# Attention and a feed-forward layer on one core: block products by seven instead of eight for the last 3072 tokens

## The chip, the cores and the metric

The kernel runs on one core of one Trainium2 chip. The metric is the device time of one execution in microseconds (us). The core has a matrix engine (TensorE, "PE"; its weight loads are listed apart as "PEld"), VectorE ("DVE"), ScalarE ("ACT"), GpSimd ("POOL") and SyncE ("SP"), which issues all the transfers of this kernel. Each engine works through its own queue in the order in which the program gives it instructions, and waits there for what an instruction needs.

## The reference

Eight batches of 576 tokens pass through attention with eight heads of width 64. Four heads look at the last 32 positions, four at the positions of the same residue modulo 32. The result, 4608 tokens by 512, goes through two matrix products with a gate between them.

```python
mask_local = (rel >= 0) & (rel < stride)                       # stride = 32
mask_strided = (rel >= 0) & (pos[None, :] % stride == pos[:, None] % stride)
...
x = attn_out.transpose(0, 2, 1, 3).reshape(B * S, H * D)       # 4608 x 512
h = x @ w_in                                                   # 512 x 2048
g = np.where(h >= 1, h, np.where(h <= -1, 0.0, (h + 1) ** 2 / 4))
return g @ w_out                                               # 2048 x 512
```

Everything is float32. The kernel gets that precision from a fast matmul type of fewer bits by splitting each operand into a high and a low part and adding three products: high by high, high by low, low by high (`HI_LO`).

## The kernel before

**Tiles.** The feed-forward layer runs over nine chunks `c` of 512 tokens, and in each over 16 blocks `f` of 128 hidden columns. `up(c, f)` makes one block of `h` by 12 matmuls of 128x128 weights against 512 tokens (four blocks of the 512 inputs by three products, line 540). `gate` makes `g` from it: a Relu with scale and bias on ACT (549), a square on ACT (550), `max(h, 1)` against that, the smaller one, on DVE (554), then the high part on ACT (556) and the low part on DVE (559). `down` adds the block into four output banks by 12 matmuls (570). All 16 blocks of both weights lie in SBUF in split form for the whole run; they are split during chunk 0 (lines 172 to 203, on ACT, DVE and POOL).

**PSUM.** Four banks hold the output sums ("o"), two the blocks of `h` ("h"), two serve attention ("a").

**Attention.** One batch is a list of named steps on four units `u`: scores `s` on PE, mask `m` and maximum `x` on DVE, `a` (subtract the maximum) on POOL (368), exponential `e` on ACT (375), sum `q` on DVE (379), `p` (add epsilon) on ACT (383), `r` (reciprocal on DVE, then a multiplication on POOL, 392), `t` (transposes of 32x32 blocks on DVE, 429), `j` (eight transfers to DRAM and one back, 443 and 444, on SP), values `v` on PE, and the high and low parts of the result, `h` on ACT (500) and `l` on DVE (504), which are written into the ring `xT` of 1536 tokens.

**Order.** The order is written out by hand, for every engine. Batches 0 and 1 are spread by `begin` and `STEPS` over the start and chunk 0. From chunk 1 on one batch is spread by `LATER` over the 16 blocks of a chunk, so that seven chunks have a batch beside them (0 to 6) and the last two none. From chunk 1 on `down` runs for two blocks at once, after the `up` of every even block: PE sees up, down of two blocks, up, up, down of two blocks, up. The gate of an odd block has the time of one `up` before its result is used.

## Time and profile before

Three runs took 881.39, 881.96 and 882.36 us (median 881.96). The profiled execution has a span of 881.9 us from its first to its last instruction, which is its own time.

| what | value |
|---|---|
| span of the profiled execution | 881.9 us |
| PE busy | 872.9 us, 99% |
| DVE busy | 384.6 us, 44% |
| ACT busy | 398.0 us, 45% |
| POOL busy | 114.7 us, 13% |
| mean granted PE clock | 0.996 of full |
| moved by DMA | 77.61 MB, mean 88 GB/s |

Busy times are sums over instructions. PE's is modelled: the end of a matmul lies after the start of the next one, so that what a matmul costs is better read from the distance of starts than from its mean duration.

### The profile page before, as it was taken

To read this page: it belongs to the slowest core of one execution; us is meant where nothing else is said; L and a number is where in the kernel's file an instruction comes from. 1 tells how busy PE (TensorE), PEld (TensorE's weight loads), DVE (VectorE), ACT (ScalarE), POOL (GpSimd) and SP (SyncE) were. 2 spreads that over 40 slices of the span, in tenths; PEclk is the share of its full clock that TensorE was granted. 3 is DMA by queue.
4 is the path that set the end of the run, shared out by engine and by line. 5 is a ranking of instruction groups with operands and counts; after the bars stand their busy time and mean duration, and the time that the engine had idled before them with its cause. 6 is when DMAs were issued, how large, how long until landed. Compare 5 with 4: busy or idle time off the path is not lost.

```text
span 881.9 us, 17353 instructions
## 1 busy us (share of the span) xinstructions
PE 872.9 (99%) x7253; PEld 710.3 (81%) x7253; DVE 384.6 (44%) x709; ACT 398.0 (45%) x732; POOL 114.7 (13%) x136
## 2 busy tenths in 40 slices
PE   8999999999999999999999999999999999999998
PEld 6788888888888888887888888888888888888886
DVE  5899854443453434434344345333453322222221
ACT  5889953434434443334434343444333433343333
POOL 6354411100120002100110011100210000000000
PEclk8999999999999999999999999999999999999999
DMA  9917331422232322421241223321222000000001
GB/s 354 405 65 242 114 121 61 140 59 60 105 100 81 83 70 72 125 64 62 81 145 52 67 105 94 87 82 49 76 82 60 33 29 1 0 35 14 1 0 48
DMA packets 41646, 77.61 MB, mean 88 GB/s; under 512 B 8800, under 2 KB 22112, under 8 KB 41568
## 3 DMA queue, kind: packets, MB, share of 16 engines
q1 hardware_dynamic: 41568, 76.50, 26.8%
q8 instruction: 57, 0.93, 0.4%
q14 instruction: 21, 0.17, 0.1%
HBM read 59.18 MB, written 17.30 MB: 87 GB/s over the span
## 4 chain that ended last, share of the span: by engine, by line
PE 95%; DMA 1%; ACT 1%; DVE 1%; SPq 1%; issue 0%; ACTq 0%; DVEq 0%
PE o L570 44%; PE h L540 44%; PE xp L459 3%; PE sc L302 3%; DMA qk<-in_qk_s 1%; PE tp L405 1%; SPq L443 0%; DMA pT<-there 0%; ACT u L549 0%; ACT u L550 0%; DMA there<-t 0%; DVE xTl L504 0%; DVE h L554 0%; SPq L237 0%; ACT gh L556 0%
## 5 line engine op out<-in xcount | busy, mean ns | idle before, releaser
L540 PE MATMUL h<-xTh,w 128*128 128x512 f32 x1152 | 373.2, 391 | 0.4 <-DVE u L554 0.4
L570 PE MATMUL o<-w,gh 128*128 128x512 f32 x1152 | 359.5, 393 | 0.1
L554 DVE SCALAR_TENSOR_TENSOR h<-h,u 128x512 f32<-128x512 f32 x143 | 100.0, 699 | 377.1 <-ACT u L550 377.0
L540 PEld LDWEIGHTS h<-xTh,w 128*128 128x128 f32 x1152 | 216.3, 188 | 46.6 <-DVE u L554 0.8
L570 PEld LDWEIGHTS o<-w,gh 128*128 128x128 f32 x1152 | 213.4, 188 | 45.3 <-ACT gh L556 0.6
L540 PE MATMUL h<-xTl,w 128*128 128x512 f32 x576 | 224.5, 390 | 0.4 <-DVE xTl L504 0.4
L570 PE MATMUL o<-w,gl 128*128 128x512 f32 x576 | 224.9, 390 | 0.0
L549 ACT ACTIVATE u<-h,half 128x512 f32<-128x512 f32 x144 | 99.1, 688 | 269.6 <-PE h L540 268.6
L559 DVE TENSOR_TENSOR gl<-h,gh 128x512 fp32r<-128x512 f32 x143 | 98.9, 692 | 84.6 <-ACT gh L556 83.7
L570 PEld LDWEIGHTS o<-w,gl 128*128 128x128 f32 x576 | 108.1, 188 | 25.7 <-DVE gl L559 0.6
L540 PEld LDWEIGHTS h<-xTl,w 128*128 128x128 f32 x576 | 108.1, 188 | 22.9 <-DVE xTl L504 1.1
L556 ACT CAST gh<-h 128x512 fp32r<-128x512 f32 x128 | 75.2, 587 | 100.1 <-DVE h L554 100.1
L550 ACT ACTIVATE u<-u 128x512 f32<-128x512 f32 x144 | 91.0, 632 | 4.6
L368 POOL TENSOR_TENSOR pr<-pr,st 128x768 f32<-128x768 f32 (+3 forms) x31 | 36.3, 1172 | 322.8 <-DVE st L364 307.6
L392 POOL TENSOR_TENSOR pr<-pr,st 128x648 f32<-128x648 f32 (+3 forms) x30 | 35.2, 1173 | 119.3 <-DVE st L391 118.4
L191 POOL TENSOR_TENSOR raw<-raw 128x512 uint32<-128x512 uint32 (+1 forms) x34 | 35.0, 1047 | 37.9 <-DVE raw L186 23.4
L504 DVE TENSOR_TENSOR xTl<-xp,xTh 128x216 fp32r<-128x216 f32 (+8 forms) x94 | 35.7, 442 | 6.0 <-ACT xTh L500 6.0
L383 ACT ACTIVATE st<-st 128x12 f32<-128x12 f32 (+2 forms) x32 | 6.8, 211 | 67.5 <-DVE st L379 67.4
L459 PEld LDWEIGHTS xp<-pT,v 64*64 64x64 f32 (+2 forms) x1760 | 29.0, 138 | 10.1 <-issue 8.2
L302 PEld LDWEIGHTS sc<-qk 64*32 64x32 f32 (+1 forms) x1856 | 25.9, 117 | 12.1 <-issue 10.1
L459 PE MATMUL xp<-pT,v 64*64 64x32 f32 (+2 forms) x1760 | 32.3, 224 | 1.5 <-DMA pT<-there 0.8
L500 ACT CAST xTh<-xp 128x216 fp32r<-128x216 f32 (+8 forms) x94 | 31.1, 459 | 6.0 <-DVE xTl L504 3.5
(56 smaller groups left out, 348.3 us busy)
## 6 DMA issues: line engine op xcount, KB each, us to landing
raw<-in_w SPq DMA_DIRECT2D x30, 512.0 KB, 9.6
qk<-in_qk_s SPq DMA_DIRECT2D x16, 604.0 KB, 4.9
qk<-in_qk_l SPq DMA_DIRECT2D x16, 576.0 KB, 4.8
out<-ob SPq DMA_DIRECT2D x35, 256.0 KB, 2.0
v<-in_v_l SPq DMA_DIRECT2D x21, 384.0 KB, 4.0
there<-t SPq DMA_DIRECT2D x96, 48.0 KB, 1.7
pT<-there SPq DMA_DIRECT2D x12, 384.0 KB, 3.0
v<-in_v_s SPq DMA_DIRECT2D x7, 384.0 KB, 4.4
```

Source lines behind the costliest of these rows:

```text
L302: nc.tensor.matmul(sc[j][i * Q:(i + 1) * Q, s, p], qk[:, 0, q0:q0 + Q], qk[:, 1, k0:k0 + W], start=u not in covered, stop=u not in covered)
L368: eng.tensor_tensor(out=pr, in0=pr, in1=st[:, 0].unsqueeze(2).broadcast_to(list(pr.shape)), op=ALU.add)
L392: eng.tensor_tensor(out=pr, in0=pr, in1=st[:, 2].unsqueeze(2).broadcast_to(list(pr.shape)), op=ALU.mult)
L459: nc.tensor.matmul(xp[p][j * D:(j + 1) * D, n], loaded[b, local, b0 + n][keys, j], qs, start=True, stop=True)
L504: nc.vector.tensor_tensor(out=dst[1], in0=src, in1=dst[0].bitcast(F32), op=ALU.subtract)
L540: nc.tensor.matmul(o_ps[c, f], wt[f][:, x, 0, cc * P:(cc + 1) * P], xT[y][:, cc, r0:r0 + CH], start=first and n == 0, stop=last and n == l ...
L549: nc.scalar.activation(u, hp, AF.Relu, bias=half, scale=0.5)
L550: nc.scalar.activation(u, u, AF.Square)
L554: nc.vector.scalar_tensor_tensor(out=g, in0=hp, scalar=1.0, in1=u, op0=ALU.max, op1=ALU.min)
L556: nc.scalar.copy(gh, g)
L559: nc.vector.tensor_tensor(out=gl, in0=g, in1=gh.bitcast(F32), op=ALU.subtract)
L570: nc.tensor.matmul(o_ps[c][t], gs[x][:, t * P:(t + 1) * P], wt[f][:, y, 1, :], start=f == 0 and n == 0, stop=f == NF - 1 and n == 2)
```

## The change

The 4608 tokens are taken as three plain chunks of 512 (`CLASSIC = 3`, c = 0, 1, 2, as before, with all weights in SBUF) and three blocks `s` of 1024 tokens.

**Blocks of 1024.** In a block both products are done by Winograd's form of Strassen's scheme: inputs and weights are cut into 2 by 2 blocks, seven products `m` of sums of blocks stand for the eight products of blocks. `up_block` goes over eight pairs `j` of hidden blocks. For each it makes seven products of 6 matmuls, in the order 1, 2, 3 of the pair before, 6, 4 of the pair before, 5, 7 (`UP`, 56 products). It adds them up in three PSUM banks (y, x, z; two sets, for even and odd `j`) and in SBUF, and puts the gate of four blocks of `g` between the products. `down_block` has 28 steps of 12 matmuls (`DOWN`), products 1, 2, 6, 7, 5, 3, 4 in this order, each over four quarters `k` of the hidden width. Before each step `prep` makes the sum of blocks of `g` where one is needed and splits it into high and low part (`split`: copy on ACT, subtraction on DVE, 1024 columns each).

**Weights.** The sums of weight blocks are made once, in chunks 1 and 2: `ship` writes three of the four split blocks of a pair to DRAM, and `combine` makes the four sums: six additions on POOL, the high part on ACT, the low part on DVE, and one transfer of 1 MB to DRAM. There are 16 combines (8 for each weight), at f = 0, 1, 2, 4, 5, 6, 8, 9, 10 of chunk 1 and f = 4, 5, 7, 8, 9, 11, 12 of chunk 2. They share one buffer `st` (and one `w32`). In the blocks each product's weights, 256 KB, come back from DRAM into a ring of seven tiles (`fetch_w`), each issued on SP when the product that used its tile is done.

**Inputs.** `x_sum` (DVE) and `x_split` (ACT and DVE) make the seven operands of a block of tokens: those of the first block in chunk 2, those of the others in the down steps of the block before (`X_NEXT`).

**Attention.** Batches start at fixed places counted in quarters of an `f`, or products (`START`), and take 42 of these instead of 64: batches 2, 3, 4 and part of 5 run in chunks 1 and 2, the rest of 5 and most of 6 in the up part of the first block, 7 in the up part of the second. The tokens of one batch are now cut at every multiple of 512 below 1536 and at 1536, 2560 and 3584.

**Output.** In `down` the weights become the stationary operand and `g` the moving one, so that the output is made transposed, 512 by 4608, and turned back on the host by a plain transposition. SBUF is given out in named slots that weights, ring, operands and blocks of `g` use one after another.

The core of the diff:

```diff
-_OUTS = [((4608, 512), "float32")]
+_OUTS = [((512, 4608), "float32")]
...
+    def combine(i, j, w32, st):
+        for f in range(2):
+            parts = [wt[2 * j + f][:, i, :, x].bitcast(F32) for x in range(2)]
+            nc.gpsimd.tensor_tensor(out=w32[:, 2 * f:2 * f + 2], in0=parts[0], in1=parts[1], op=ALU.add)
...
+        for to, a, b, op in ((0, block(1, 0), block(1, 1), ALU.add), (1, s_[0], block(0, 0), ALU.subtract),
+                             (2, block(0, 0), block(1, 0), ALU.subtract), (3, block(0, 1), s_[1], ALU.subtract)):
+            nc.gpsimd.tensor_tensor(out=s_[to], in0=a, in1=b, op=op)
+        hi, lo = st[:, :, :HF], st[:, :, HF:]
+        nc.scalar.copy(hi.bitcast(F32R), lo.bitcast(F32))
+        nc.vector.tensor_tensor(out=lo.bitcast(F32R), in0=lo.bitcast(F32), in1=hi.bitcast(F32), op=ALU.subtract)
+        nc.sync.dma_start(kept[i][j][1].rearrange("p n x e -> p n (x e)"), st)
...
     def down(*units):
...
-                    nc.tensor.matmul(o_ps[c][t], gs[x][:, t * P:(t + 1) * P], wt[f][:, y, 1, :],
+                    nc.tensor.matmul(o_ps[c][d], wt[f][:, 1, h, x, e:e + P], gs[y],
...
+    def fetch_w(n):
+        if n < len(seq):
+            i, j, m = seq[n]
+            ring[n] = short(RING_AT[n % WR], F32R, f"wr_{n}", (P, 2, HF))
+            which, at = FACTOR[m]
+            nc.sync.dma_start(ring[n].bitcast(F32), kept[i][j][which][:, at])
...
+        for n, (j, m) in enumerate(UP):
...
+            for c in range(2):
+                for q, (a, b) in enumerate(HI_LO):
+                    nc.tensor.matmul(to, w_[:, a, c * P:(c + 1) * P], xc[m][:, b, c],
...
+            fetch_w(done - 1 + WR)
+            if m == 1:
+                last = (gb[(j - 1) // 2][:, 1, (j - 1) % 2], tmp[j - 1][:, 1]) if j else None
+                if last:
+                    bent(last[1], last[0])
+                nc.scalar.copy(g11, y[j])
+                if last:
+                    squared(last[1])
+                    gated(last[0], *last)
+            elif m == 2:
+                nc.vector.tensor_tensor(out=g11, in0=x.pop(j), in1=g11, op=ALU.add)
+                bent(ua, g11)
+                squared(ua)
+            elif m == 3:
+                nc.vector.tensor_tensor(out=g12, in0=z.pop(j), in1=g12, op=ALU.add)
+                bent(ub, g12)
+            elif m == 6:
+                nc.scalar.copy(g12, y[j])
+                gated(g11, g11, ua)
+                if j:
+                    last = ga[(j - 1) // 2][:, 1, (j - 1) % 2], tmp[j - 1][:, 1]
+                    squared(last[1])
+                    gated(last[0], *last)
+            elif m == 4:
+                h = y.pop(j)
+                bent(ua, h)
+                squared(ua)
+                gated(g21, h, ua)
...
+    def prep(s, n):
+        m, k = DOWN[n]
+        hl[n] = t = slot(HL_AT[n % 3], [P, 2, 2, CH], F32R, f"hl_{s}_{n}")
+        b11, t3, b21, b22 = ga[k][:, 0], ga[k][:, 1], gb[k][:, 0], gb[k][:, 1]
+        if m == 5:
+            nc.vector.tensor_tensor(out=t3, in0=b22, in1=b11, op=ALU.subtract)
+        elif m == 4:
+            nc.vector.tensor_tensor(out=b21, in0=b21, in1=b11, op=ALU.subtract)
+        split(t, {1: b11, 6: b11, 5: t3, 7: t3, 3: b22, 2: b21, 4: b21}[m])
...
+        START = {2: 0, 3: 33, 4: 69, 5: 112, 6: 150, 7: 240}
+        LATER = {0: ("s0", "m0 x0 a0"), 3: ("", "e0"), 6: ("s1", "q0 p0 r0 m1 x1 a1"), 9: ("", "t0 j0 e1"),
+                 12: ("s2", "q1 p1 r1 m2 x2 a2"), 15: ("", "t1 j1 e2"), 18: ("v0", "h0 l0"),
+                 21: ("s3", "m3 x3 a3 q2 p2 r2"), 24: ("", "t2 j2 e3"), 28: ("", "q3 p3 r3"),
+                 33: ("v2", "h2 l2 t3 j3"), 42: ("V1", "h1 l1 h3 l3")}
```

More of the change, by code (lines that the diff above doesn't have):

```diff
@@ L140, in tile_sparse_attention_then_ffn, with x_tile @@
     nc.gpsimd.memset(half, 0.5)
-    xT = [const.tile([P, NC, RING], F32R, name=f"xT{s}") for s in "hl"]
+    xq = [slot(f"X{c}", [P, 2, NC, CH], F32R, f"xq_{c}") for c in range(2)]
+    xs = {}
+    def x_tile(s):
+        if s not in xs:
+            xs[s] = slot(f"X{s % 2}", [P, NC, 2 * CH], F32, f"xs_{s}")
+        return xs[s]
     wt, raws, pieces, held = {}, {}, {}, set()
@@ L560, in gate, with put @@
         return gh, gl
+    def put(rows, cols, t):
+        nc.sync.dma_start(out[rows * P:(rows + 1) * P, cols:cols + CH], t)
     def down(*units):
@@ L571, in down @@
                                      start=f == 0 and n == 0, stop=f == NF - 1 and n == 2)
             if f1 == NF - 1:
-                end = (c, t) == (NCH - 1, CH // P - 1)
-                for e, cols in enumerate((slice(0, 384), slice(384, DM)) if end else (slice(0, DM),)):
-                    n = cols.stop - cols.start
-                    ob = (s_p if end else o_p).tile([P, n], F32, tag="s" if end else "ob", name=f"ob_{c}_{t}_{e}")
-                    nc.scalar.copy(ob, o_ps[c][t][:, cols])
-                    nc.sync.dma_start(out[c * CH + t * P:c * CH + (t + 1) * P, cols], ob)
+                ob = o_p.tile([P, CH], F32, tag="ob", name=f"ob_{c}_{d}")
@@ L666, in tile_sparse_attention_then_ffn @@
                         fetch_qk(2, 0)
-                if post:
-                    go(post)
-                n = 2 if 0 < c and (c, f) < (NCH - 1, NF - 1) else 1
+                go(post)
+                if c:
+                    steps(g0, g0 + 2, 1)
+                    ship(f, c - 1)
+                    if (c, f) in COMBINE:
+                        i, j = COMBINE[c, f]
+                        if c == 1:
+                            w32, st = (x_tile(0)[:, :, e0:e1] for e0, e1 in ((704, 960), (192, 704)))
+                        else:
+                            w32, st = (slot(X_AT[m], [P, 4, n], F32, f"{a}_{j}") for m, n, a in ((3, HF, "w32"), (4, CH, "st")))
+                        combine(i, j, w32, st)
+                    if c == 2:
+                        x_steps(0, *X_FIRST.get(f, ()))
+                n = 2 if c else 1
                 if len(pend) > 2:
```

309 lines of the change are left out of this document (253 added, 56 removed), and 3 rows, old and new, of the table LATER.

## The prediction

> **What bounds the kernel now.** First the page: busy shares, bytes per slice, the four large matmul groups.
>
> ```profile
> span 881.9 us, 17353 instructions
> PE 872.9 (99%) x7253; PEld 710.3 (81%) x7253; DVE 384.6 (44%) x709; ACT 398.0 (45%) x732; POOL 114.7 (13%) x136
> ...
> GB/s 354 405 65 242 114 121 61 140 59 60 105 100 81 83 70 72 125 64 62 81 145 52 67 105 94 87 82 49 76 82 60 33 29 1 0 35 14 1 0 48
> ...
> L540 PE MATMUL h<-xTh,w 128*128 128x512 f32 x1152 | 373.2, 391 | 0.4 <-DVE u L554 0.4
> L570 PE MATMUL o<-w,gh 128*128 128x512 f32 x1152 | 359.5, 393 | 0.1
> ...
> L540 PE MATMUL h<-xTl,w 128*128 128x512 f32 x576 | 224.5, 390 | 0.4 <-DVE xTl L504 0.4
> L570 PE MATMUL o<-w,gl 128*128 128x512 f32 x576 | 224.9, 390 | 0.0
> ```
>
> PE is never short of work. The means overlap, so I take a matmul's price from the chain of waits in order of time, and that of a chunk from windows over line 570, one with an attention batch beside it and one without.
>
> ```profile
> 782.08 5.44 PE h L540 x24
> ```
> ```profile
> 172.97:268.98 96.01, 45.41 (x193) 1.00 0.29 85
> 782.08:869.40 87.32, 45.05 (x193) 1.00 0.03 13
> ```
>
> A matmul costs 5.44/24 = 0.2267 us, an up or a half of a down (12) 2.72, a batch 96.0 - 87.3 = 8.7 us of PE. Then the timeline of one gate, which shows how much room there is:
>
> ```profile
> 781.92 0.39 PE L540 MATMUL h<-xTh,w 128*128 128x512 f32 x1
> ...
> 784.90 0.69 ACT L549 ACTIVATE u<-h,half 128x512 f32<-128x512 f32 x1 [5.47 <-PE h L540]
> ...
> 786.28 0.70 DVE L554 SCALAR_TENSOR_TENSOR h<-h,u 128x512 f32<-128x512 f32 x1 [6.13 <-ACT u L550]
> ...
> 787.02 0.59 ACT L556 CAST gh<-h 128x512 fp32r<-128x512 f32 x1 [0.76 <-DVE h L554]
> ...
> 787.64 0.69 DVE L559 TENSOR_TENSOR gl<-h,gh 128x512 fp32r<-128x512 f32 x1 [0.66 <-ACT gh L556]
> ...
> 788.38 0.19 PEld L570 LDWEIGHTS o<-w,gl 128*128 128x128 f32 x1
> ```
>
> The odd block's up ends at 781.92 + 2.72 = 784.64; ACT starts 0.26 later and the gate takes 3.4 (784.90 to 788.33). PE fetches the low part at 788.38, as it appears: an odd gate has no slack. An even one has until the second next up, 8.16 - 0.26 - 3.4 = 4.5 us.
>
> **What is removed.** Before: 1152 + 1152 + 576 + 576 = 3456 matmuls. After: three chunks of 384 and three blocks of 56 x 6 + 28 x 12 = 672, together 3168. 288 fewer are 65.3 us; attention's matmuls stay. With everything else hidden: 881.9 - 65.3 = 816.6. The rest asks how much of this the queues give back.
>
> **The combines (chunks 1 and 2).** Prices of the new shapes come from the groups by form:
>
> ```profile
> L392 POOL TENSOR_TENSOR pr<-pr,st 128x768 f32<-128x768 f32 x7 | 10.3, 1476 | 5.5 <-DVE st L391 5.5
> L392 POOL TENSOR_TENSOR pr<-pr,st 128x384 f32<-128x384 f32 x7 | 5.8, 834 | 36.6 <-DVE st L391 36.6
> ```
> ```profile
> L201 DVE TENSOR_TENSOR w<-raw,w 128x512 fp32r<-128x512 f32 x30 | 19.4, 684 | 0.0
> L392 DVE TENSOR_TENSOR pr<-pr,st 128x768 f32<-128x768 f32 x1 | 1.0, 957 | 0.0
> ```
> ```profile
> L550 ACT ACTIVATE u<-u 128x512 f32<-128x512 f32 x144 | 91.0, 632 | 4.6
> L375 ACT ACTIVATE pr<-pr 128x768 f32<-128x768 f32 x8 | 6.8, 846 | 2.0 <-POOL pr L368 2.0
> ```
>
> By straight lines: POOL 0.62 us for 256 columns and 1.05 for 512; 1024 columns 1.23 on DVE, 1.06 on ACT. For the transfers (KB, us to landing; then one spread `j` on SP's timeline, whose last row is the price of one issue):
>
> ```profile
> out<-ob SPq DMA_DIRECT2D x35, 256.0 KB, 2.0
> ...
> qk<-in_qk_s SPq DMA_DIRECT2D x16, 604.0 KB, 4.9
> ```
> ```profile
> 177.94 3.61 SPq L443 DMA_DIRECT2D there<-t  x8
> 182.92 0.34 SPq L444 DMA_DIRECT2D pT<-there  x1
> ```
>
> 1 MB lies between 2.0 us plus 768 KB at the page's 405 GB/s (3.9) and 4.9 in proportion (8.3); I take 4.5, because the 604 KB loads go out in pairs that share the engines. There is one `st`, so the combines form a ring: copy on ACT 1.06, low part on DVE 1.23, issue 0.35, landing 4.5, four POOL additions 2.5, handovers 0.3, together 9.9 us. The copy stands in ACT's queue ahead of the next gate, and PE waits for that. A block `f` lasts 87.3/16 plus 3.4 batches x 8.7 over 32 blocks: 6.4 us. The first combine also waits on POOL for `a0` (1.48), two additions (2.1) and four (2.5), then copies: 7.1 behind its gate. Chunk 1: 7.1 + 8 x 9.9 = 86 against 10 blocks, 64: 22 late, less the 4.5 an even gate may wait: 18. Chunk 2: 7.1 + 6 x 9.9 = 66 against 8 blocks, 51: less 4.5, 11. So at least some 29. Laying the queues out block by block, with odd gates that have no slack and with combines behind `a` and `r` of the same slot, I get 41 for chunk 1, and 7/9 of it, 32, for chunk 2. From below: a landing of 3.9, queued POOL work done early and both gates tolerant leave 10. I take 40 of 10 to 73, nearer 29, since the layout takes each wait at its longest.
>
> **Up parts.** Gate prices, besides the 632 above:
>
> ```profile
> L554 DVE SCALAR_TENSOR_TENSOR h<-h,u 128x512 f32<-128x512 f32 x143 | 100.0, 699 | 377.1 <-ACT u L550 377.0
> ...
> L549 ACT ACTIVATE u<-h,half 128x512 f32<-128x512 f32 x144 | 99.1, 688 | 269.6 <-PE h L540 268.6
> ...
> L556 ACT CAST gh<-h 128x512 fp32r<-128x512 f32 x128 | 75.2, 587 | 100.1 <-DVE h L554 100.1
> ```
>
> Seven products are 9.52 us of PE. Product 1 of pair j+1 overwrites the bank that the gate after product 4 of j-1 reads. Following ACT and DVE from product 1 (1.36, then 0.26): copy, square, gated, sum, bent, square, bent, copy, square, bent, square, gated is 2 x 0.59 + 4 x 0.63 + 2 x 0.70 + 0.69 + 2 x 0.63 + 0.69 = 7.7 and twelve handovers of 0.03: 9.7 us. So a bare period loses 0.2, 4 over 21 periods (0 to 6).
>
> Attention comes on top, about 2.45 batches in the up parts (0.6, 0.85, 1). Its groups on ACT, and ACT's wait for DVE inside it from the view of waits (us, times, longest):
>
> ```profile
> L375 ACT ACTIVATE pr<-pr 128x768 f32<-128x768 f32 (+3 forms) x32 | 22.2, 694 | 2.0 <-POOL pr L368 2.0
> ...
> L383 ACT ACTIVATE st<-st 128x12 f32<-128x12 f32 (+2 forms) x32 | 6.8, 211 | 67.5 <-DVE st L379 67.4
> ...
> L500 ACT CAST xTh<-xp 128x216 fp32r<-128x216 f32 (+8 forms) x94 | 31.1, 459 | 6.0 <-DVE xTl L504 3.5
> ```
> ```profile
> ACT st L383 <- DVE st L379: 67.4, 26, 4.0
> ```
>
> Per batch 60.1/8 = 7.5 us of work, and 67.4/26 = 2.6 us of waiting at each of four `p`: up to 18 us in a queue that is now PE's clock, against the 8.7 that PE has for itself. That is 0 to 9 a batch, 0 to 23; I take half, 12.
>
> **Weights from DRAM.** A tile is issued when a product ends and is needed six products later, 8.16 us; less 0.35 and 2.0 for landing 5.8 remain. Ahead of it on SP now stand the spreads. By the two rows of SP above one holds it for 5.3 us (177.94 to 183.26), after it has waited for DVE's transposes. Ten fall into up parts (batch 5 two, 6 and 7 four each). With 2.5 us for the transposes each is 2 late, less attention's own PE time: 0 to 25 in all, I take 5, because a PE that is late for other reasons gives the ring its time.
>
> **Down parts.** A step is 2.72 us. For products 5 and 4 `prep` is serial, sum, copy, low part: 1.23 + 1.06 + 1.23 + 0.1 = 3.6. Four steps of product 5 with one sum and one split for the next block between them take 17.0 of DVE against 10.9; the steps before leave a lead of 1.8: 4.3 lost in two blocks, 0.5 in the last. Product 4 with two output sums: 16.0 against 10.9, lead 3.3: 1.8 in each. Together 14 (6 to 20). Where up turns to down, the third operand waits for the last gate (its slot is `tmp`): 1.4 a block; with the first ring tiles and the two early splits, 6 (2 to 12).
>
> **Small parts.** Batch 0 is now cut at token 512: eight more high parts in the start, where PE waits for them.
>
> ```profile
> L500 ACT CAST xTh<-xp 128x36 fp32r<-128x36 f32 x12 | 3.5, 288 | 0.0
> ```
>
> 8 x 0.29 = 2 us (0 to 4). In `down` the low part is needed one matmul earlier, 0.23 a pair; most of it lies inside the combines' stalls: 1 (0 to 4). The split order of the weights and the transposed output change no count.
>
> **Sum.** 816.6 + 40 + 4 + 12 + 5 + 14 + 6 + 2 + 1 = 900.6. The median stands 0.06 above the span: 901 us, 19 more than before.
>
> **Rivals.** *The queues hold (faster).* If the combines' ring is shorter than a block and a third (8.5 us: landing 3.9 and POOL additions that start while the transfer runs), PE never feels them. For it speaks that DVE and ACT stand at 44% and 45%; against it, that one buffer is waited for by three engines in turn. Then 10 remain of the 40, and of the other 44 about half, since PE's own lateness then no longer piles up from stage to stage: 816.6 + 10 + 22 = 849. The sign turns where all stalls together reach 65.
>
> *The clock falls.* My layout leaves PE idle for 4 to 8 us before odd gates. At the start PE had a thin stretch, and the granted clock (the number behind the brackets) followed:
>
> ```profile
> 14.00:16.00 2.00, 1.03 (x8) 0.82 (x8) 2.00 (x5) 1.98 (x5) 0.66 (x1) 1.00 1.00 377
> ...
> 18.00:20.00 2.00, 1.70 (x31) 1.23 (x27) 0.64 (x3) 1.41 (x4) 0.65 (x1) 0.50 1.04 422
> ...
> 22.00:24.00 2.00, 2.00 (x12) 1.96 (x11) 1.95 (x5) 1.07 (x4) 0.74 (x1) 0.65 1.04 417
> ```
>
> Some 6 us at half clock lose 3. Ten such gaps are 30, of which a part lies in stalls anyway: 901 + 25 = 926. [...]
>
> *The ring starves.* Spreads, loads of q, k and v and 193 GB/s of tiles (256 KB per 1.36 us) share one queue: at the upper ends of ring and attention, 901 + 20 + 11 = 932. Against it: the page's 405 GB/s.
>
> *The matmuls don't get fewer in time.* If changing banks every six matmuls or streaming `g` costs what is saved, 0.02 us on each of 3168 matmuls, 63 us: 882 if no queue stalls. The up of today changes its bank every 12 without loss.
>
> **Chances.** Forecast 0.42 (885 to 915), queues hold 0.27 (835 to 879), clock 0.17, ring 0.10, no gain on PE 0.04. Under 0.2% (1.8 us) this kernel's runs tell nothing. Faster 0.28, the first rival and a little; same 0.03; slower 0.69. The range takes in most of the first rival and reaches the two slow ones: 843 to 938; the forecast's own is 885 to 915.
>
> **What would show it.** Right: in the windows of chunks 1 and 2, 384 matmuls take 20 us more than 96; ACT's copy in `combine` waits for POOL, POOL's third addition for the transfer; in down, DVE's low part waits for ACT and PE for DVE. Wrong: a chunk with combines at 96 us; PE waiting for ring tiles above all; a granted clock under 1 in chunks 1 and 2; products that start more than 1.36 us apart in the last block.

## The result, and the profile after

The kernel after took 988.14 us (median of 4, 987.04 to 992.65) beside 881.67 us (881.27 to 882.36) for the kernel before: 1.121 times the time, 95% interval 1.119 to 1.124, or 106 us more. The forecast was 901 us, its range 843 to 938: the sign was right, the size was not.

First the page of the kernel after: span, busy times, and in the slices PE's busy share and granted clock in tenths.

```profile
span 985.3 us, 17928 instructions
PE 857.5 (87%) x6965; PEld 679.3 (69%) x6965; DVE 555.8 (56%) x822; ACT 495.7 (50%) x852; POOL 236.7 (24%) x244
...
PE   8999967767698865868889798998889989999997
...
PEclk8999988969799997989999899999999999999999
```

The 288 matmuls are gone (7253 to 6965), yet the span grew. PE has holes in slices 6 to 27 above all, and its clock dips there too; from slice 34 on it is as dense as before. In windows by stage this is chunks 1 and 2 (first row), the up parts of the three blocks (the next three, the third without attention), and then five rows of 2 us around the first combine. After the length of the window stand PE, PEld, DVE, ACT and POOL, each busy time with the number of instructions, then granted clock, DMA share and GB/s.

```profile
124.60:436.30 311.70, 234.65 (x2270) 183.13 (x2268) 127.85 (x212) 105.52 (x197) 128.06 (x133) 0.87 0.53 174
441.90:551.40 109.50, 95.95 (x985) 74.35 (x985) 60.55 (x102) 65.83 (x118) 20.70 (x16) 0.96 0.75 244
639.50:741.70 102.20, 91.97 (x801) 72.00 (x800) 52.05 (x87) 59.22 (x105) 17.42 (x13) 0.95 0.65 199
825.00:901.50 76.50, 76.47 (x338) 63.03 (x337) 37.98 (x55) 52.48 (x87) 7.22 (x3) 1.00 0.68 200
...
136.00:138.00 2.00, 0.71 (x4) 0.24 (x2) 0.00 (x0) 0.00 (x0) 1.92 (x3) 1.00 0.00 0
138.00:140.00 2.00, 0.00 (x0) 0.00 (x0) 0.00 (x0) 0.00 (x0) 1.92 (x4) 1.00 0.00 0
140.00:142.00 2.00, 0.00 (x0) 0.00 (x0) 0.24 (x1) 1.32 (x2) 1.92 (x3) 0.50 0.00 0
...
152.00:154.00 2.00, 1.60 (x3) 1.07 (x4) 1.37 (x2) 1.29 (x2) 0.00 (x0) 0.50 0.00 0
...
156.00:158.00 2.00, 2.00 (x8) 1.59 (x7) 1.90 (x6) 0.86 (x2) 2.00 (x2) 0.73 1.03 357
```

From 124.6 us on, chunks 1 and 2 hold 31 ups of 2.72 us, 17 double downs of 5.44 and 3.4 batches of 8.7, together 206. They took 312: 105 us lost, where the prediction had 40. An up part has 56 products of 1.36, 76.2 us, and 8.7 for each batch beside it (1.45, 1 and none); beyond that the three lost 26 (with 5.6 between the last plain matmul and the first product), 17 and 0.3 us. The down parts took 88.1, 83.2 and 79.7 against 76.2, which is 22 more. 816.6 + 105 + 43 + 22 is 987, within 2 of the span.

The timeline of the first combine (start, duration, engine, line; in brackets the wait just before and its releaser; some rows in between left out) shows what a late sum does:

```profile
133.68 3.03 PE L599 MATMUL h<-xq,w 128*128 128x512 f32 x12
133.74 1.47 POOL L409 TENSOR_TENSOR pr<-pr,st 128x768 f32<-128x768 f32 x1 [19.62 <-PE sc L343]
135.17 2.52 POOL L244 TENSOR_TENSOR xs<-w 128x512 f32<-128x512 f32 x2
137.76 2.88 POOL L252 TENSOR_TENSOR xs<-xs 128x256 f32<-128x256 f32 x4
140.68 1.04 ACT L254 CAST xs<-xs 128x1024 fp32r<-128x1024 f32 x1 [9.73 <-POOL xs L252]
141.63 1.55 ACT L644 COPY ob<-o 128x512 f32<-128x512 f32 x3
141.75 1.32 DVE L255 TENSOR_TENSOR xs<-xs 128x1024 fp32r<-128x1024 f32 x1 [8.16 <-ACT xs L254]
142.26 0.80 PE L640 MATMUL o<-gh,w 128*128 128x512 f32 x1 [5.56 <-ACT ob L644]
143.10 0.62 SPq L256 DMA_DIRECT2D ks<-xs  x1
143.82 5.55 SPq L629 DMA_DIRECT2D out<-ob  x4
147.76 2.89 POOL L252 TENSOR_TENSOR xs<-xs 128x256 f32<-128x256 f32 x4 [3.56 <-DMA ks<-xs]
148.43 0.58 ACT L644 COPY ob<-o 128x512 f32<-128x512 f32 x1 [5.25 <-DMA out<-ob]
151.76 0.58 ACT L622 CAST gh<-h 128x512 fp32r<-128x512 f32 x1 [0.77 <-DVE h L609]
152.40 0.80 PE L640 MATMUL o<-gh,w 128*128 128x512 f32 x1 [8.49 <-ACT gh L622]
```

ACT stands 9.73 us at the combine's copy. Behind it are the copies that empty the output banks of chunk 0, and PE waits 5.56 us for a bank. The four output transfers stand in SP's queue behind the combine's 1 MB, which waits for DVE; the last `ob` copy waits 5.25 for a free buffer, the next gate stands behind it, and PE waits 8.49 us more. One combine cost 14 us of PE time. From 136.71 PE was idle; from 140 the clock is at half, and after 152.4 it took until about 157 to come back: the fall came 3.3 us after PE stopped, and the return 4.7 us after it went on.

A much shorter hole of this trace, too, was followed by a fall: PE stood for 2.03 us (294.80 to 296.83), and the clock was at half from 297.0 to 300.4. In rows of 2 us, PE's busy time and the granted clock (1.00, 1.00, 0.55, 0.59, 1.00):

```profile
292.80:294.80 2.00, 2.00 (x9) 1.31 (x7) 0.00 (x0) 0.00 (x0) 0.00 (x0) 1.00 0.62 228
294.80:296.80 2.00, 0.00 (x0) 0.00 (x0) 0.00 (x0) 1.79 (x4) 0.00 (x0) 1.00 0.28 101
296.80:298.80 2.00, 1.72 (x96) 1.49 (x96) 0.74 (x2) 1.64 (x3) 0.00 (x0) 0.55 0.99 296
298.80:300.80 2.00, 2.00 (x16) 1.56 (x6) 1.35 (x3) 0.58 (x1) 0.00 (x0) 0.59 0.47 130
300.80:302.80 2.00, 2.00 (x10) 1.62 (x10) 1.97 (x4) 0.07 (x1) 0.00 (x0) 1.00 0.21 43
```

In the whole stretch PE was idle for 311.70 - 234.65 = 77 us; busy time times (1 - clock) over windows of 2 us gives another 23 lost to the clock. The kernel before has neither in the same 312 us of its time:

```profile
124.60:436.30 311.70, 310.93 (x2692) 253.34 (x2694) 129.37 (x245) 127.29 (x234) 33.02 (x33) 1.00 0.28 86
```

The view of waits of the kernel after (us, times, longest):

```profile
ACT xs L254 <- POOL xs L252: 51.8, 8, 11.3
...
ACT st L254 <- POOL st L252: 36.0, 6, 9.7
...
PE o L640 <- ACT gh L622: 23.1, 7, 8.5
...
PE sc L343 <- DVE xq L563: 16.7, 3, 9.8
...
PE xp L500 <- DMA pT<-there: 11.4, 2, 9.9
...
PE z L722 <- DMA wr<-ks: 8.2, 3, 3.3
PE y L722 <- DMA wr<-kq: 7.3, 2, 5.6
PE y L722 <- DMA wr<-ks: 7.2, 3, 2.9
```

ACT stood 88 us at the copies of 14 combines. PE waited not only for gates (23.1) but also with attention's own matmuls at the head of its queue: scores for a bank (16.7), values for the spread probabilities (11.4). What the new instructions cost, by form, and what the new transfers took to land:

```profile
L244 POOL TENSOR_TENSOR xs<-w 128x512 f32<-128x512 f32 x18 | 25.7, 1449 | 0.2
L252 POOL TENSOR_TENSOR xs<-xs 128x256 f32<-128x256 f32 x36 | 25.6, 731 | 12.5 <-DMA ks<-xs 11.3
```
```profile
kq<-w SPq DMA_DIRECT2D x48, 256.0 KB, 4.0
ks<-xs SPq DMA_DIRECT2D x9, 1024.0 KB, 5.3
ks<-st SPq DMA_DIRECT2D x7, 1024.0 KB, 5.0
```

### The profile page after: what moved, and what is told of

Its sections match the earlier page's. It is cut to its first block, busy times and chain, and to the rows that moved or that the text cites. A ratio compares the mean times of both kernels' runs of the same rounds, so it can differ in the third digit from the quotient of the medians.

```text
span 985.3 us, 17928 instructions
## 1 busy us (share of the span) xinstructions
PE 857.5 (87%) x6965; PEld 679.3 (69%) x6965; DVE 555.8 (56%) x822; ACT 495.7 (50%) x852; POOL 236.7 (24%) x244
## 4 chain that ended last, share of the span: by engine, by line
PE 44%; DVE 16%; DMA 12%; ACT 11%; POOL 9%; issue 5%; SPq 3%; ACTq 0%; DVEq 0%; POOLq 0%
PE y L722 9%; PE yo L828 8%; PE h L599 6%; PE o L640 6%; DMA wr<-ks 5%; PE z L722 4%; DVE hl L691 4%; PE xo L828 3%; ACT hl L690 3%; PE xp L500 2%; POOL xs L252 2%; PE x L722 2%; SPq L484 2%; POOL st L252 2%; DMA there<-t 2%
## 5 line engine op out<-in xcount | busy, mean ns | idle before, releaser
L722 PE MATMUL y<-x,wr 128*128 128x512 f32 x576 | 148.1, 404 | 20.2 <-DMA wr<-kq 7.3
L640 PE MATMUL o<-gh,w 128*128 128x512 f32 x384 | 134.9, 418 | 28.7 <-ACT gh L622 23.1
L599 PE MATMUL h<-xq,w 128*128 128x512 f32 x576 | 148.8, 410 | 3.7 <-DVE gl L625 2.8
L722 PEld LDWEIGHTS y<-x,wr 128*128 128x128 f32 x576 | 109.7, 194 | 49.6 <-DVE gb L609 6.2
L828 PE MATMUL yo<-hl,wr 128*128 128x512 f32 x576 | 136.9, 395 | 7.4 <-DVE hl L691 4.7
L599 PEld LDWEIGHTS h<-xq,w 128*128 128x128 f32 x576 | 111.8, 198 | 30.2 <-DVE gl L625 3.2
L828 PEld LDWEIGHTS yo<-hl,wr 128*128 128x128 f32 x576 | 108.6, 190 | 34.0 <-DVE hl L691 7.8
L640 PEld LDWEIGHTS o<-gh,w 128*128 128x128 f32 x384 | 76.7, 200 | 49.3 <-ACT gh L622 26.4
L722 PE MATMUL z<-x,wr 128*128 128x512 f32 x288 | 75.8, 400 | 8.3 <-DMA wr<-ks 8.2
L640 PE MATMUL o<-gl,w 128*128 128x512 f32 x192 | 79.7, 415 | 1.1 <-DVE gl L625 1.1
L343 PE MATMUL sc<-qk 64*32 64x64 f32 (+1 forms) x1856 | 35.6, 242 | 23.7 <-DVE xq L563 16.7
L500 PE MATMUL xp<-pT,v 64*64 64x32 f32 (+2 forms) x1760 | 35.2, 234 | 22.1 <-DMA pT<-there 11.4
```

The lines of the kernel that those rows point to most:

```text
L343: nc.tensor.matmul(sc[j][i * Q:(i + 1) * Q, s, p], qk[:, 0, q0:q0 + Q], qk[:, 1, k0:k0 + W], start=u not in covered, stop=u not in covered)
L500: nc.tensor.matmul(xp[p][j * D:(j + 1) * D, n], loaded[b, local, b0 + n][keys, j], qs, start=True, stop=True)
L599: nc.tensor.matmul(o_ps[c, f], wt[f][:, 0, h, x, e:e + P], xq[c][:, y, cc], start=first and n == 0, stop=last and n == len(todo) - 1)
L640: nc.tensor.matmul(o_ps[c][d], wt[f][:, 1, h, x, e:e + P], gs[y], start=f == 0 and n == 0, stop=f == NF - 1 and n == 2)
L722: nc.tensor.matmul(to, w_[:, a, c * P:(c + 1) * P], xc[m][:, b, c], start=m in (1, 2, 5) and c + q == 0, stop=c == 1 and q == 2, skip_grou ...
L828: nc.tensor.matmul(to, w_[jj][:, a, d * P:(d + 1) * P], t[:, b, jj], start=m in (1, 2, 5) and k + jj + q == 0, stop=k == NP // 2 - 1 and j ...
```

## The experiments

All start from the kernel after. Each was run twice beside three runs of the kernel before (medians 881 to 883 us), the last, e20, five times beside eight. Stages are read from the first matmul of each in the timeline: "plain" is chunks 1 and 2, from 124.6 us in every run. The first matmul of chunk 1 lay between 118.3 and 120.7 us, so that differences of some 2 us in that column can come from ahead of it.

| run | us | ratio to before, 95% | plain | up, down of block 0 | block 1 | block 2 |
|---|---|---|---|---|---|---|
| after | 988.1 | 1.119 to 1.124 | 312 | 109.5, 88.1 | 102.2, 83.2 | 76.5, 79.7 |
| e1_late_end | 980.3 | 1.103 to 1.121 | 308 | 111.4, 90.1 | 99.7, 83.0 | 76.5, 79.7 |
| e5_sums_stay | 968.4 | 1.089 to 1.104 | 291 | 112.1, 88.3 | 100.2, 83.0 | 76.5, 79.7 |
| e11_late_and_stay | 931.3 | 1.052 to 1.061 | 254 | 114.0, 88.3 | 99.9, 83.0 | 76.5, 79.6 |
| e2_no_sums | 925.1 | 1.044 to 1.054 | 246 | 111.6, 90.0 | 103.7, 83.3 | 76.5, 80.0 |
| e10_few_bytes | 907.1 | 1.017 to 1.038 | 231 | 115.2, 89.2 | 100.4, 83.0 | 76.5, 79.7 |
| e14_few_bytes_slots | 900.6 | 1.017 to 1.023 | 224 | 115.1, 88.2 | 98.8, 83.0 | 76.5, 79.6 |
| e3_gate_ring | 979.0 | 1.106 to 1.115 | 300 | 115.0, 88.3 | 100.9, 83.0 | 76.5, 79.7 |
| e4_spread_apart | 985.4 | 1.113 to 1.122 | 324 | 111.5, 83.9 | 96.3, 83.3 | 76.5, 79.7 |
| e7_no_spread | 952.7 | 1.074 to 1.084 | 312 | 99.0, 83.8 | 88.6, 83.3 | 76.5, 79.7 |
| e12_spread_pool | 982.3 | 1.111 to 1.118 | 310 | 120.6, 84.8 | 97.7, 83.0 | 76.5, 79.7 |
| e6_batch7_down | 985.1 | 1.110 to 1.121 | 310 | 112.9, 111.6 | 76.5, 83.0 | 76.5, 79.7 |
| e8_sum_ahead | 977.6 | 1.106 to 1.112 | 314 | 113.0, 83.8 | 100.5, 77.7 | 76.5, 77.7 |
| e13_four_edits | 950.9 | 1.074 to 1.084 | 296 | 115.1, 79.2 | 96.9, 77.8 | 76.5, 77.7 |
| e15_all_out | 870.0 | 0.983 to 0.988 | 242 | 98.6, 78.5 | 88.5, 77.7 | 76.5, 77.7 |
| e18_three | 940.6 | 1.061 to 1.073 | 280 | 113.1, 83.1 | 98.6, 77.7 | 76.5, 77.7 |
| e16_three_flip5 | 907.0 | 1.023 to 1.035 | 277 | 98.9, 78.3 | 89.2, 77.8 | 76.6, 77.7 |
| e17_three_flip2 | 906.3 | 1.024 to 1.032 | 276 | 101.4, 78.3 | 89.3, 78.0 | 76.6, 77.6 |
| e20_halves_dve | 903.4 | 1.022 to 1.028 | 276 | 100.3, 78.3 | 89.1, 77.7 | 76.5, 77.7 |

### What the sums cost

**e1_late_end** ends each combine (copy, low part, transfer) one block later, so that ACT need not wait for POOL.

```diff
             nc.gpsimd.tensor_tensor(out=s_[to], in0=a, in1=b, op=op)
-        hi, lo = st[:, :, :HF], st[:, :, HF:]
+        ends.append((i, j, st))
+    def combine_end():
+        ...
+        i, j, st = ends.pop()
+        hi, lo = st[:, :, :HF], st[:, :, HF:]
...
+                    combine_end()
                     if (c, f) in COMBINE:
```

> The last part of each combine (copy on ACT, low part on DVE, transfer) is given out one block later, behind the next gate, so that POOL has a whole block for its additions. Theory one, ACT's queue is held by POOL's additions: ACT's waits for POOL in combine fall from 52 + 36 us to under 30, chunks 1 and 2 (124.6 to 436.4, 312 us) shrink by 40 to 60 us, the time to about 930 to 950. Rival, the single buffer sets the pace (copy, low part, 1 MB out, additions, about 11 us for each of 16): the order changes little, 970 to 990. Rival, attention twice as dense makes PE wait for it: the same, 970 to 990.

The stretch gained 4 us. The one buffer still closes the ring: its transfer now starts later, and POOL's waits for it grew from 21 to 70 us (11.3 and 10.0, then 41.4 and 28.2, for its two places `xs` and `st`).

**e2_no_sums** makes no sums at all.

```diff
-                        combine(i, j, w32, st)
+                        for r in range(2):
+                            nc.sync.dma_start(kept[i][j][1][:, 2 * r:2 * r + 2], wt[2 * j + r][:, i].bitcast(F32))
```

> The sums of weight blocks are left out: six additions on POOL, copy on ACT and low part on DVE are not made; the same number of bytes goes to DRAM straight from the weights (two transfers of 512 KB in place of one of 1 MB), so the second product's numbers are not the reference's. Theory one, the combines cost the chunks their time: chunks 1 and 2 fall from 312 us to about 215 to 235 and the granted clock there returns to 1.0; time about 895 to 910. Rival, dense attention: chunks 1 and 2 stay above 265, time above 940. Rival, the bytes to DRAM: no change at all.

66 us of the 105 go; 39 stay.

**e3_gate_ring** numbers the slots of `gh` and `gl` through over the chunks: they restarted at 0 in each, so that the first gate of a chunk waited for the down just before it. The weight ring's first tiles, which take these slots over, are renumbered to match.

```diff
-((6, F32, "u"), (f % 3, F32R, "gh"), (3 + f % 3, F32R, "gl"))
+((6, F32, "u"), ((16 * c + f) % 3, F32R, "gh"), (3 + (16 * c + f) % 3, F32R, "gl"))
...
-RING_AT = (1, 4, 6, 2, 5, 0, 3)
+RING_AT = (0, 3, 6, 1, 4, 2, 5)
```

> The three slots of gate outputs go on counting over the chunks (16 c + f modulo 3) instead of starting again at f = 0, so that the first block of a chunk does not take the slot of the block just before it. Theory: ACT's copy of the first gate of chunks 1 and 2 no longer waits for the down of the block before (5.5 us at 124.9); as the first combine follows behind it, 5 to 15 us less, 973 to 983. Rival, hidden behind the wait for POOL at the same place: no change, 985 to 990.

12 us of the plain stretch, 9 of the whole.

**e5_sums_stay** makes the sums, but the buffer is not what is sent, so it is free when DVE is done.

```diff
-        nc.sync.dma_start(kept[i][j][1].rearrange("p n x e -> p n (x e)"), st)
+        for r in range(2):
+            nc.sync.dma_start(kept[i][j][1][:, 2 * r:2 * r + 2], wt[2 * j + r][:, i].bitcast(F32))
```

> All the sums of weight blocks are made as in the changed kernel, but what goes to DRAM is read from the weights (the same bytes, so the second product's numbers are not the reference's). Their buffer is then free again when DVE has made the low part, without waiting for a transfer. Theory, the single buffer with its transfer sets the pace of the combines: chunks 1 and 2 fall from 312 us by 25 to 45. Rival, POOL's additions in front of ACT's copy are enough to hold the queues: under 12 us less. With the sums left out altogether it was 246 us.

The stretch gained 21 us. **e11_late_and_stay** has the edits of e1 and e5 together:

> Two edits together: the end of each combine is given out one block later, and what goes to DRAM is read from the weights (numbers not the reference's), so that neither POOL's additions nor a transfer of the buffer stand in front of ACT's copy. Theory, the two waits stand in for each other, and the late end does something only when the buffer is free: chunks 1 and 2 fall to 250 to 270 us, near the 246 without sums. Rival, the work itself (POOL 5.4, ACT 1.05, DVE 1.23 us for each of 16 and attention's places behind it on POOL) costs the time: 280 or more, near the 291 of the free buffer alone.

4 and 21 us alone, 58 together: the wait for POOL and the wait for the transfer stand in for each other, and one is only worth something once the other is gone. Against e2 the work of the sums itself, all of which e11 still does, is 7 us.

**e10_few_bytes** is e2 with only the first pair's blocks written and read back for all; **e14_few_bytes_slots** adds the edit of e3.

```diff
-            if n != (1, 0):
+            if n != (1, 0) and j == 0:
...
-                        for r in range(2):
+                        for r in range(2 if j == 0 else 0):
...
-            nc.sync.dma_start(ring[n].bitcast(F32), kept[i][j][which][:, at])
+            nc.sync.dma_start(ring[n].bitcast(F32), kept[i][0][which][:, at])
```

> Without the sums, as in the run that left them out, and in addition only the first pair's blocks of each weight go to DRAM (3.5 MB instead of 28) and are read again for every pair; numbers are not the reference's. Theory, dense attention in its own queues makes chunks 1 and 2 late by the 40 us that stay without the sums (246 against 206 worked out): still above 235 us. Rival, the writes hold SP and the transfers of attention: 210 to 220.

> As the run with few bytes to DRAM and no sums, and in addition the gate's slots count on over the chunks. Theory, of what is left in the plain part (its end at 355 us, 331 worked out with full cover) some 10 to 12 us are the first gates of chunks 1 and 2 that wait for the slot of the block before: end at 343 to 347. Rival, all of it is dense attention in PE's own queue: 352 or more.

Writing takes 16 us of the stretch, the slots another 7. So one ladder leads down from 312: 58 for the waits of the sums, 7 for their work, 16 for the writes, 7 for the slots; 17 remain over the 206: 13 us of idle PE, 4 of them at gates and most of the others at attention's own matmuls, and the clock. The steps depend on their order (the slots are worth 12 on top and 7 at the end).

### The spreads in the up parts

**e4_spread_apart** issues the eight transfers of a spread two places after the transposes, and the transfer back three or four places after the eight, so that SP does not stand there.

```diff
-            nc.sync.dma_start(pT[:, :, :n], there)
+            back[u] = pT[:, :, :n], there
+        def gather(u):
+            nc.sync.dma_start(*back.pop(u))
```

> For batches 2 to 7 the eight transfers of a spread are given out two products after the transposes, and the transfer back three products after that, so that SP does not stand waiting for either. Theory, the spreads hold back the weight tiles in the up parts: up of the first two blocks falls from 109 and 102 us to 92 to 97 and 86 to 92, the waits of PE for tiles nearly vanish, 20 to 30 us less in all, about 960. Rival, attention's work on ACT and DVE makes the up parts late, the tiles only show it: 980 to 990.

The blocks gained 14 us (with the gap before them), but the plain stretch lost 12: PE now waits for the late transfer itself, 48 us in that stretch and in all

```profile
PE xp L506 <- DMA pT<-there: 57.7, 14, 16.3
```

**e7_no_spread** sends no probabilities of batches 5 to 7.

```diff
+            if b >= 5:
+                nc.gpsimd.memset(pT[:, :, :n], 0.0)
+                flipped[u] = pT
+                return
```

> Batches 5, 6 and 7 leave the nine transfers of a spread out; POOL fills the transposed probabilities with zeros instead (their tokens' output is not the reference's). All other work of attention stays. Theory, the spreads hold SP and with it the weight tiles: up of the first two blocks falls from 109 and 102 us to 92 and 87 or less, PE's waits for tiles vanish. Rival, attention's work and waits on ACT and DVE set the time: both stay above 100 and 95.

35 us go: 10 and 14 in the two up parts, the 5.6 before them, 4 in the first down.

**e12_spread_pool** keeps the spreads and lets POOL issue them from batch 5 on.

```diff
-                    nc.sync.dma_start(to, ts[h][i * ST:(i + 1) * ST, :, :n])
-            nc.sync.dma_start(pT[:, :, :n], there)
+                    (nc.gpsimd if b >= 5 else nc.sync).dma_start(to, ts[h][i * ST:(i + 1) * ST, :, :n])
+            (nc.gpsimd if b >= 5 else nc.sync).dma_start(pT[:, :, :n], there)
```

> The nine transfers of each spread of batches 5, 6 and 7 are issued by POOL instead of SP; nothing is left out. Theory, they hold back the weight tiles by holding SP: up of the first two blocks falls to about 100 and 89 us, as when the spreads were left out, 30 us less in all, about 955. Rival, it is their bytes and small packets in the shared engines: up stays above 105 and 98.

Only 6 us. PE no longer waits for weight tiles, and the 5.6 us ahead of the first block are gone, but its up part is 11 us longer than in the kernel after. The DMA view and the waits of this run (KB and us to landing; us, times, longest):

```profile
there<-t SPq DMA_DIRECT2D x48, 48.0 KB, 1.7
pT<-there SPq DMA_DIRECT2D x6, 384.0 KB, 3.4
there<-t POOLq DMA_DIRECT2D x48, 48.0 KB, 2.9
pT<-there POOLq DMA_DIRECT2D x6, 384.0 KB, 4.9
```
```profile
PE xp L500 <- DMA pT<-there: 19.7, 6, 9.7
```

The rows of SP and those of POOL are of different stages, since SP's are batches up to 4. In the two up parts of the kernel after, SP's 48 KB took 2.8 and 1.7 us to land and its transfer back of 384 KB 3.2 and 3.1, beside POOL's 2.9 and 4.9 here. PE waits 20 us for what they bring instead of 11; 9.9 of it lie in the two blocks, where the kernel after has none. And a spread now holds POOL: the eight are issued from 481.13 to 485.39, the transfer back at 489.41, 4.02 us after POOL began to wait for the eight, and the additions and multiplications behind it wait as weight tiles did on SP. So the spreads cost about 35 us, but in more ways than one: they hold the queue that issues them, and the values wait for them. Moving the issue trades the one queue for the other; how much each way costs is not separated.

### The down parts, and batch 7

**e8_sum_ahead** makes the sum that `prep` needs one step earlier, so that DVE's sum, ACT's copy and DVE's low part are no longer one chain.

```diff
         m, k = DOWN[n]
+        if n + 1 < len(DOWN):
+            first_sum(n + 1)
...
-        if m == 5:
-            nc.vector.tensor_tensor(out=t3, in0=b22, in1=b11, op=ALU.subtract)
-        elif m == 4:
-            nc.vector.tensor_tensor(out=b21, in0=b21, in1=b11, op=ALU.subtract)
```

> In the down parts the sum of blocks that products 5 and 4 need is made by DVE one step earlier, ahead of the split of the step before, so that sum, copy and low part of one step no longer follow each other within it. Theory, this serial chain (3.6 us in a step of 2.7) is what the down parts lose: down of the second block from 83.2 to 78 to 80, of the third from 79.7 to 77 to 78, of the first 3 to 5 less; 8 to 10 us in all. Rival, weight tiles or the gates behind the turn set it: under 2 us.

The three down parts gain 11.8 us and stand at 83.8, 77.7 and 77.7 against 76.2. DVE's wait for ACT's copy, in the kernel after and then here:

```profile
DVE hl L691 <- ACT hl L690: 62.6, 58, 5.5
```
```profile
DVE hl L691 <- ACT hl L690: 41.5, 47, 6.4
```

**e6_batch7_down** moves batch 7 from the second up part to the down part before it.

```diff
-        START = {2: 0, 3: 33, 4: 69, 5: 112, 6: 150, 7: 240}
+        START = {2: 0, 3: 33, 4: 69, 5: 112, 6: 150, 7: 194}
```

> Batch 7 starts at place 194 instead of 240, so that all of it lies in the down part of the first block and none in the up part of the second. Theory, attention's own work (8.7 us of PE) and what its waits do to the queues make an up part late: up of the second block falls from 102 us to 76 to 79, as in the third block, where there is no attention either. Down of the first block, with steps twice as long and without gates, takes 10 to 16 more than its 88: about 10 to 15 us less in all. Rival, an up part late for the traffic of weight tiles alone: up of the second block stays above 90.

The up part falls from 102.2 to 76.5, the down part rises from 88.1 to 111.6: the batch costs 23 to 26 us in either, not the 8.7 of PE alone. Its two windows, the down part with the batch and the up part without:

```profile
552.00:664.00 112.00, 94.39 (x911) 74.10 (x902) 77.82 (x91) 46.63 (x74) 14.77 (x11) 0.94 0.64 204
664.00:740.00 76.00, 75.97 (x336) 62.56 (x335) 38.39 (x55) 52.52 (x87) 7.20 (x3) 1.00 0.64 201
```

### The causes together

**e13_four_edits** has the edits of e1, e3, e8 and e12, **e15_all_out** those of e11, e7, e3 and e8.

> Four edits that leave the result whole: the end of a combine one block later, gate slots that count on, spreads of batches 5 to 7 from POOL, sums of the down parts one step ahead. If the causes are separate the gains add: 8 + 9 + 32 + 9 us, about 930. It stays slower than the kernel before, since 16 combines through one buffer and dense attention in chunks 1 and 2 remain.

> All the causes found are taken out at once: combines that end one block later and whose buffer waits for no transfer (DRAM gets the weights' own bytes), gate slots that count on, no spreads for batches 5 to 7 (zeros instead), sums of the down parts one step ahead. Numbers are not the reference's. If the causes are the right ones and separate, 988 - 57 - 35 - 9 - 11 = 876, and the seven products would only then be worth about what their stalls cost. Rival, the causes stand in for each other and something else takes their place: over 900.

The four edits of e13 gave 37 us and not the 58 expected, since e12's, counted there as 32, is worth 6. In e15, with the waits named so far taken out, the program, which still does all the sums and all the block products, takes 870 us: 1.2 to 1.7% less than before. It is no usable version: the sums do not reach DRAM, and batches 5 to 7 have no probabilities. Its plain stretch:

```profile
124.60:366.70 242.10, 215.91 (x2263) 171.99 (x2261) 128.03 (x211) 106.63 (x197) 133.84 (x135) 0.94 0.66 224
```

and what PE waits for longest in it:

```profile
PE xp L513 <- issue: 14.5, 4, 7.9
```

54 of the 170 us lost remain: 36 in this stretch, 13 in the up parts, 5 in the down parts. The profile names no releaser for the largest wait, that of the value matmuls. But three of its four pieces, 13.7 us, lie in this stretch, and each ends 0.09 us after the landing of a transfer back, for the spreads of batches 2 to 4, which this run keeps. The longest:

```profile
177.65 0.34 SPq L498 DMA_DIRECT2D pT<-there  x1
...
181.23 1.56 PE L513 MATMUL xp<-pT,v 54*64 54x64 f32 x48 [7.90 <-issue]
```

This transfer landed at 181.14. So the value matmuls still wait for spreads here.

### Towards a version that keeps everything

**e18_three** cuts the combine into three parts (two additions; four; copy, low part and transfer), each half a block of `f` after the one before it, with a combine every 1.4 to 1.5 blocks, and has the edits of e3 and e8. **e16_three_flip5** also turns the probabilities of batches 5 to 7 by transposes on PE, as batch 1 did, so that nothing of these batches is spread through DRAM; **e17_three_flip2** does so from batch 2 on (by the order of its program, batch 3 then writes its tokens over the columns of the last combine's buffer in chunk 1 before they are read, so part of its output is another).

```diff
-    def combine(i, j, w32, st):
+    def combine_add(i, j, w32):
...
+    def combine_sub(i, w32, st):
...
+    def combine_end(i, j, st):
...
-        COMBINE = {(1, 4 * n // 3): (n >= NP, n % NP) for n in range(NP + 1)}
-        COMBINE |= {(2, 3 + 4 * n // 3): (1, n) for n in range(1, NP)}
+        COMBINE = {(1, 11 * n // 4): (int(n >= NP), n % NP) for n in range(NP + 1)}
+        COMBINE |= {(2, 3 + 3 * n): (1, n) for n in range(1, NP)}
...
-                for at, names in LATER.items():
+                for at, names in (FLIPS if b >= 5 else LATER).items():
```

> The combines in three parts, gate slots that count on and sums one step ahead, with all spreads as in the changed kernel. It tells the share of the plain part from that of the transposes: plain part ends at 370 to 390, up parts stay at 110 to 115 and 100, time about 910.

> A whole result again. Each combine is taken apart in three: two additions on POOL, four additions half a block later, copy, low part and transfer another half block later, combines one and a half blocks apart, so that neither ACT nor POOL stands waiting for the buffer. Gate slots count on; sums of the down parts one step ahead; batches 5 to 7 turn their probabilities by PE transposes and a copy on DVE, as batch 1 does, in place of DVE transposes and nine transfers. Theory, the causes are waits and not work: the plain part ends at 365 to 385 instead of 436 us, up of the first two blocks takes 100 and 92, the time is 875 to 895, at the kernel before. Rival, transposes and their banks make PE wait in the up parts as much as the tiles did: up stays above 108 and 98, time above 900.

> The same, with the PE transposes for all batches from 2 on. Theory, in chunks 1 and 2 the values also wait for the transfer back (11 us of PE's waits there) and SP for the spreads: the plain part ends 5 to 15 us earlier than with the spreads of batches 2 to 4 left, 865 to 885. Rival, 20 transposes a batch and four more turns of the two attention banks cost more than the transfers did: 5 to 15 us later.

All three plain stretches ended at 400 to 405 us, later than the expected 365 to 390. The blocks of e16 are as short as those of e15, which has no spreads there: PE's transposes cost 28 us less than the spreads (e18's blocks take 526.7 us together, e16's 498.5). The plain stretch stays at 277, and transposing more batches (e17) does not change it. **e20_halves_dve** then gives each half of a block's input tile its own slot, so that a batch does not wait for a combine's buffer, and puts the four additions on DVE.

```diff
-            nc.gpsimd.tensor_tensor(out=s_[to], in0=a, in1=b, op=op)
+            nc.vector.tensor_tensor(out=s_[to], in0=a, in1=b, op=op)
...
-    def x_tile(s):
+    def x_half(s, c):
...
-                    rooms_[i, j] = [x_tile(0)[:, :, e0:e1] for e0, e1 in ((704, 960), (192, 704))]
+                    rooms_[i, j] = [x_half(0, 0)[:, :, 256:], x_half(0, 1)]
```

> A whole result, on top of the run with combines in three parts and PE transposes for batches 5 to 7. First, the input tiles of the blocks are cut into halves of 512 tokens, each with a slot of its own, and the combines of chunk 1 use a half that no batch writes yet as their buffer; in that run ACT's high parts of batch 2 waited 12.4 us for the buffer's transfers, though they write other columns of the same tile, and PE then 27.8 us for scores whose banks those high and low parts hold. Second, the four additions into the buffer are made by DVE (about 0.4 us each) right ahead of ACT's copy, a block and a half after the transfer before. Theory, these false waits and POOL's waits for the buffer are most of the 70 us that the plain part still loses: it ends at 360 to 380 instead of 402, time 865 to 885, level with the kernel before or a little under it. Rival, dense attention itself holds PE: the plain part ends after 390, time over 895.

The same 276 us. Its waits:

```profile
ACT st L258 <- DVE st L254: 27.4, 7, 7.2
ACT xs L258 <- DVE xs L254: 27.0, 9, 5.7
...
PE sc L347 <- DVE xq L568: 11.2, 3, 8.9
PE sc L347 <- ACT xs L559: 11.2, 5, 8.2
ACT xs L559 <- DMA ks<-xs: 10.4, 1, 10.4
```

ACT still waits 54 us, now for DVE; attention's writes still wait for a combine's transfer, and PE for the banks that they read. Of the 48 us of PE's waits in the plain stretch 42 come ahead of attention's own matmuls (scores, values and transposes) and the rest mostly at gates. So the rival expected for this run, that dense attention holds PE and the stretch ends after 390, came nearer than the theory: it ended at 400. No version that computes everything beats the kernel before; the best, this one, is 2.2 to 2.8% slower. Whether another order would is open.

## Why the prediction was right or wrong

**The base, 816.6: right.** Without attention a block's up part took 76.5 us against 76.2, so a product costs its 6 x 0.2267, and the rival in which the matmuls gain nothing is out. The 4 us for bare up periods were not there (0.3).

**The combines, 40 of 10 to 73: the step that failed.** The stretch lost 105 us. The ring's own parts were nearly right: in the first turn 1.04 + 1.32 + 4.66 to the next addition + 2.89 is 9.9 us, as worked out, though an addition of 512 columns cost 1.45 us on POOL and not 1.05 (the rows it was drawn from had other operands), one of 256 0.73 and not 0.62. What was wrong is the comparison with blocks of a fixed 6.4 us and the waits on gates alone. A late combine delays the next gate, and besides it the copies out of the banks, SP's transfers behind its own, and attention's writes, for which PE stands at scores and values in the order of its queue; each of these makes the block longer, and the next gate later. The layout counted gates, and from the layout's 73 I went down towards the 29 that the bare ring gave. e11 against e2 shows that it is waiting (58) and not work (7). The slots of `gh` and `gl`, which restart with each chunk, were in no term: 7 to 12. Of the writes to DRAM, together 16 by e10 against e2, the prediction had the landing of the sums but not those of `ship` (4.0 us to land).

**The clock, a rival at 926: it came, but on top.** 23 of the 105 us are the clock, and some 10 more in the blocks (4 and 5 in the two up parts with attention). It is no alternative to stalls but a surcharge on them: 23 us on 77 idle in the plain stretch of the kernel after (mean granted clock 0.87), 14 on 27 in e2 (0.93), 9 on 26 in e15 (0.94). It belonged into the sum.

**Weight ring 5 and attention 12: the first far too small, the second about right.** With the spreads of batches 5 to 7 gone 35 us go (e7), of which some 30 lie in the up parts; the rival "the ring starves" had the mechanism and 31 us for it. What the up parts of e15 still lose, 10 + 4, is set against the attention term of 12 as a remainder; PE's waits there are for gates (5.0 for DVE, 2.5 for ACT), which fits the mechanism, but no run took attention's waits on ACT away alone. With 6 for the turns the up parts were given 27 us and lost 43.

**Down parts 14 (6 to 20): right in mechanism, too small at 22.** The chain of sum, copy and low part was 11.8 (e8); the other 10 of the 22 are the tail of batch 6 in the first down part (4, gone in e7) and small waits.

**Start 2, order of the low part 1:** not to be seen; the stages close to 2 us without them.

**"The queues hold": wrong,** by 77 us of idle PE. But e15 shows where it would have led: 870 us, not the 849 worked out, even with the sums still made.

## What to carry to other kernels

When a new step stands in several in-order queues, its price is not the time by which its ring exceeds a block: list everything behind it on each engine, the transfers and the matrix engine's own side work too, and let the block grow by that before comparing again. Two waits in series may each look cheap when removed alone (4 and 21 us) and be worth 58 together. Where the matrix engine's stream gets holes, put the clock into the sum and not among the rivals: here it cost 23 us on 77 idle, 14 on 27 and 9 on 26, and a hole of 2.03 us was followed by a fall to half (0.50).

## What was not expected of the hardware

An addition on POOL with two full operands cost 1.45 us for 512 columns in pieces of 256, as much as 1.47 for 768 columns in attention's line 409. Transfers of 384 KB that POOL issued (e12, batches 5 to 7) took 4.9 us to land, those that SP issued in the two up parts of the kernel after 3.2 and 3.1. And the granted clock fell to half (0.50) 3.3 us into the hole from 136.7 to 152.4, in which there are three matmuls, and took another 4.7 us of busy time to return, so that the hole cost PE more than its length.
